# Even token blocks, weight sums on GpSimd and one more product summed in PSUM, in a kernel of attention and two dense layers

## The chip, the cores and the metric

The kernel runs on one core of a Trainium2 chip. The metric is the device time of one execution in microseconds (us). The profile names the engines PE (TensorE, matmuls), PEld (its weight loads), DVE (VectorE), ACT (ScalarE), POOL (GpSimd) and SP (SyncE, which issues nearly all DMAs here).

## The reference

Attention in two steps with batch 8, 8 heads, 576 tokens, head size 64 and 32 packed queries: `p_packed = softmax(p k^T) v`, then `out = softmax(q p_packed^T) p_packed`. The result is laid out as 4608 tokens of 512 values and goes through two blocks of the same shape, 512 to 2048 and back to 512:

```python
h = x @ w_in;  x = (h * np.cos(h)) @ w_out            # first block: layers one and two
h = x @ w2_in; g = h * np.tanh(np.log1p(np.exp(h)))   # second block: layers three and four
out = g @ w2_out
```

The second block's function is the activation that the kernel calls Mish. The weights of both blocks come as 64-bit floats and are turned into 32-bit ones in the kernel (an activation on ScalarE, a shift and a shift-or on VectorE).

## The kernel before

Every 32-bit product is made of three matmuls of a rounded type, high x high, high x low and low x high (`mm3`, L141). So each operand is split: ScalarE copies it to the rounded type, and VectorE or GpSimd subtracts that copy from it to get the low part.

**First part (L792 to L940).** The tokens run in 16 tiles of 288, each with 16 steps of 128 hidden columns, 256 steps in all. Step n does `l1(n)` (layer one into a PSUM bank of a ring of four), a chain on ScalarE and VectorE for h cos h (L809 to L833, the low part on GpSimd in L832), and `l2(n - 3)` (layer two into four accumulators). Attention, conversions of weights and preparations of the second block stand in tables `bg_pe`, `bg_ew` and `bg_ld` by step and are run between. One of these preparations is `wo2_pair` (L585): for each of eight pairs of 128 rows of w2_out it loads 64-bit data into two `raw` tiles, converts them (`conv2`), forms four differences in place (`sums`, L628, on VectorE), splits seven pieces (`piece`, L619 and L620) and writes each to DRAM (`tst`). Its steps are listed as offsets from a start step.

**Second part (L942 to L1138).** Layers three and four are each done with seven products of half-size blocks in place of eight (the Strassen-Winograd scheme). The tokens run in blocks: four of 1024 and one of 512 tokens, so that a half block has 512 or 256 columns (`n`). Per block, `x_load`, `x_sums` and `x_split` bring the seven combinations of x. They stand in the program behind the block before (`xs`, 18 units) and are let in one at a time between two groups.

For each of eight pairs of hidden columns (`p`), a block makes seven products for layer three (`product`, L947: six matmuls of `n` columns, `ps<-wab,ws` in the trace). K3 (L72) gives their order. The banks come from the ring of four, and VectorE adds them up (L1099, L1119) while ScalarE applies Mish. The third product is summed in PSUM on top of the first. The seven weight combinations of a pair are made in block 0: `comb_sums` (L556), then `ws_load` (L569), which splits the piece (L576 on ScalarE, L577 on VectorE, or on GpSimd for k = 2 and 5) and writes it to DRAM; later blocks load it from there. `ws_load` runs five products ahead, in five buffers that it shares with other temporary tiles.

Layer four has 56 groups per block (`group`, L1048), seven kinds `k` times eight `p`, each of two halves of three matmuls (`acc<-gh,T` in the trace). A group's operand is prepared by a possible sum (L1062) and a split (L961 on ScalarE, L962); its weights `T` are loaded from the pieces of `wo2_pair`, eight ahead. After each product one half of a group is taken from the queue (`sub`); behind the eight `p` the rest is done two halves at a time, until 28 halves are left over for the next block, and all of them in the last. After the eighth group of a kind `post` adds the bank to a sum (L1041) or writes a quarter of the result (L1015 transposes, L1018 DMAs).

The order on each engine isn't the program's order: the framework runs a timeline simulation of its own and issues each instruction at the place where that simulation has it ready, by priority. Each engine then executes its queue in that fixed order.

Of the kernel before, what the change touches and what calls it, by code (L numbers as in the profile page):

```python
# [12 lines left out]
ALU = mybir.AluOpType  # L13
# [57 lines left out]
HP_W = 400  # L71
K3 = (0, 2, 1, 3, 4, 5, 6)  # L72
K4 = (2, 7, 4, 5, 3)
# [11 lines left out]
def build(tc, q, k, v, p, w1i, w1o, w2i, w2o, out):  # L85
    nc = tc.nc
    ctx = ExitStack()
    with ctx:
# [480 lines left out]
        def ws_load(m):  # L569
            if m >= NQ:  # L570
                return
            p, k = divmod(m % 56, 7)
            k = K3[k]
            w = WS[m] = tp.tile([128, 2, 2, 128], F32R, tag="tmp", bufs=TMP_BUFS, name=nm("ws"))
            if m < 56:
                nc.scalar.copy(w[:, 0], CB[p][k])  # L576
                (nc.gpsimd if k % 3 == 2 else nc.vector).tensor_tensor(w[:, 1], CB[p][k], w[:, 0], ALU.subtract)  # L577
                d = WST[(p, k)] = dram.tile([128, 2, 2, 128], F32, name=nm("wst"))
                nc.sync.dma_start(d, w.bitcast(F32))
            else:  # L580
                nc.sync.dma_start(w.bitcast(F32), WST[(p, k)])
# [3 lines left out]
        def wo2_pair(p):  # L585
# [26 lines left out]
            def half(x, h):  # L612
                return raw[x][:, 256 * h : 256 * h + 256, 1].bitcast(F32)
# [12 lines left out]
            def sums(x, h, a, b):  # L626
                def f():
                    nc.vector.tensor_tensor(half(x, h), half(*a), half(*b), ALU.subtract)  # L628

                return f  # L630
# [4 lines left out]
                    (2, conv2(0)),  # L635
                    (3, conv2(1)),
                    (4, piece(1, 0, 0)),
                    (4, piece(2, 1, 0)),
                    (5, piece(3, 1, 1)),
                    (6, sums(0, 0, (0, 1), (0, 0))),  # L640
                    (6, sums(0, 1, (1, 1), (0, 1))),
                    (7, sums(1, 1, (1, 1), (0, 0))),
                    (7, sums(1, 0, (1, 0), (1, 1))),
                    (7, piece(5, 0, 0)),
                    (8, piece(7, 0, 1)),
                    (8, piece(6, 1, 1)),
                    (9, piece(4, 1, 0)),
                ],
# [212 lines left out]
        def x_load(i, a):  # L861
            def f():
                n = 1024 if i < 4 else 512
                if i == 0:
# [4 lines left out]
                for r, kc in zip(rs, (a, 2 + a)):  # L869
                    lo, hi = 1024 * i, 1024 * i + n  # L870
                    for t in range(lo // TT, (hi - 1) // TT + 1):
# [6 lines left out]
        def x_sums(i, a):  # L878
            def f():
                n = 512 if i < 4 else 256  # L880
                b1, b2 = raws[(i, a)]
# [10 lines left out]
        def x_split(i, a, k):  # L892
            def f():
                n = 512 if i < 4 else 256
                if a == 0:
# [104 lines left out]
        def block(i, n):  # L1000
            B = {"G": {}}
            r0 = 1024 * i

# [44 lines left out]
            def group(k, p):  # L1048
# [3 lines left out]
                def prep():  # L1052
# [12 lines left out]
                    g["hl"] = bp.tile([128, 2, BT], F32R, tag="gh2", bufs=4, name=nm("gh2"))  # L1065
                    split(g["hl"], src, n, nc.gpsimd if n < 512 and p % 4 == 3 else nc.vector)

# [20 lines left out]
            for p in range(8):  # L1088
# [20 lines left out]
                add(u3, prod(3), u2)  # L1109
                c = add(gb[:, 0, :n], prod(4), u3)  # L1110
                nc.scalar.activation(c, c, AF.Mish)
                ps = prod(5)
                a22 = add(ga[:, 1, :n], ps, u3)
                nc.scalar.activation(a22, a22, AF.Mish)
                add(u2, ps, u2)
                a21 = add(gb[:, 1, :n], prod(6), u2)
                nc.scalar.activation(a21, a21, AF.Mish)
# [10 lines left out]
        for i in range(NBLK):  # L1128
            n = 512 if i < 4 else 256
            xs = x_units(i + 1) if i < 4 else []  # L1130
# [31 lines left out]
```

## Time and profile before

| | us |
|---|---|
| median of three runs | 1584.92 |
| lowest, highest | 1582.02, 1586.48 |
| the profiled execution | 1589.55 |
| its span, first to last instruction | 1587.8 |
| mean granted TensorE clock, share of full speed | 0.981 |

The profile gives each engine's busy time, and the trace every instruction with its start, duration and what ended the idle time before it (`<-`). Matmuls overlap in a pipeline: a row's duration is longer than the distance to the next start. The second part begins at about 848 us. A window's row counts matmuls that touch the window.

### The profile page before, as it was taken

How to read it: one execution, taken by the hardware profiler on the slowest of the kernel's cores; microseconds unless marked ns; L12 is line 12 of the kernel's file. 1: busy time of each engine (PE TensorE's matmuls, PEld its weight loads, DVE VectorE, ACT ScalarE, POOL GpSimd, SP SyncE). 2: the span in 40 equal slices, each digit the busy share in tenths (PEclk: the TensorE clock that was granted, in tenths of full speed). 3: DMA queues.
4: the chain of work that ended last, by engine and by line, in shares of the span. 5: the costliest groups of instructions: out<-in, count | busy, mean ns of one | idle time of the engine just before them, and what ended most of it. 6: DMA issues, size and time to landing. Idle time of an engine off the chain costs nothing.

```text
span 1587.8 us, 28508 instructions
## 1 busy us (share of the span) xinstructions
PE 1488.5 (94%) x9728; PEld 1262.8 (80%) x9728; DVE 1159.0 (73%) x2284; ACT 895.9 (56%) x1822; POOL 423.4 (27%) x452
## 2 busy tenths in 40 slices
PE   3789999999998999999999989999999999999987
PEld 1577787799886899788998767888788878878877
DVE  4986767777677776687765889875986598657846
ACT  3676677666666677667665755433543444344433
POOL 0562323334443444456541112000100110010001
PEclk9889999999999999999999999999999999999999
DMA  9889666544547444532205858676867677767977
GB/s 282 284 217 226 174 160 161 136 125 111 150 125 193 121 122 126 153 115 69 96 16 180 255 204 254 209 222 194 249 206 221 203 225 214 217 199 228 273 256 245
DMA packets 243920, 294.45 MB, mean 185 GB/s; under 512 B 104000, under 2 KB 129088, under 8 KB 243776
## 3 DMA queue, kind: packets, MB, share of 16 engines
q1 hardware_dynamic: 243776, 292.63, 63.7%
q8 instruction: 77, 1.26, 0.3%
q14 instruction: 67, 0.55, 0.1%
HBM read 239.08 MB, written 53.48 MB: 184 GB/s over the span
## 4 chain that ended last, share of the span: by engine, by line
PE 55%; DVE 10%; DMA 6%; ACT 4%; issue 4%; POOL 1%; SPq 1%; DVEq 0%; POOLq 0%; ACTq 0%
PE acc L143 10%; PE acc L142 10%; PE acc L144 10%; PE ps L142 8%; PE ps L143 8%; PE ps L144 8%; DVE gh L962 1%; DMA xr<-x2d 1%; DVE r L815 1%; PE ps L488 1%; DMA tst<-wt 1%; DMA T<-tst 1%; DMA ws<-wst 1%; DVE t L1062 1%; DMA raw<-in_moe_w_in_dram 1%
## 5 line engine op out<-in xcount | busy, mean ns | idle before, releaser
L832 POOL TENSOR_TENSOR gh<-r,gh 128x288 fp32r<-128x288 f32 x256 | 214.6, 846 | 348.7 <-ACT gh L829 243.6
L143 PE MATMUL acc<-gh,wo 128*128 128x288 f32 x1024 | 302.6, 302 | 2.8 <-POOL gh L832 2.7
L144 PE MATMUL acc<-gh,wo 128*128 128x288 f32 x1024 | 299.4, 299 | 0.0
L142 PE MATMUL acc<-gh,wo 128*128 128x288 f32 x1024 | 277.9, 305 | 1.8 <-ACT gh L829 1.8
L142 PE MATMUL ps<-wab,ws 128*128 128x512 f32 (+1 forms) x560 | 209.4, 375 | 12.8 <-ACT m L1105 4.5
L142 PEld LDWEIGHTS acc<-gh,wo 128*128 128x128 f32 x1024 | 183.8, 192 | 32.3 <-ACT gh L829 9.0
L143 PE MATMUL ps<-wab,ws 128*128 128x512 f32 (+1 forms) x560 | 207.9, 371 | 0.8 <-DVE wab L899 0.8
L144 PE MATMUL ps<-wab,ws 128*128 128x512 f32 (+1 forms) x560 | 207.5, 371 | 1.0 <-DVE ws L577 1.0
L143 PE MATMUL acc<-gh,T 128*128 128x512 f32 (+1 forms) x560 | 206.5, 372 | 0.8 <-DVE gh L962 0.7
L143 PEld LDWEIGHTS acc<-gh,wo 128*128 128x128 f32 x1024 | 195.0, 191 | 14.5 <-issue 7.4
L144 PE MATMUL acc<-gh,T 128*128 128x512 f32 (+1 forms) x560 | 205.0, 370 | 0.0
L144 PEld LDWEIGHTS acc<-gh,wo 128*128 128x128 f32 x1024 | 195.1, 191 | 7.3 <-issue 7.3
L142 PE MATMUL acc<-gh,T 128*128 128x512 f32 (+1 forms) x560 | 179.7, 374 | 8.9 <-ACT gh L961 7.2
L821 ACT ACTIVATE r<-r,halfpi 128x288 f32<-128x288 f32 x256 | 136.1, 535 | 90.8 <-DVE r L815 89.5
L142 PE MATMUL ps<-aT,wab 128*128 128x288 f32 x512 | 161.4, 315 | 20.4 <-DVE r L822 18.1
L822 DVE TENSOR_TENSOR r<-r,ps 128x288 f32<-128x288 f32 x256 | 114.8, 450 | 72.9 <-ACT r L821 71.6
L812 ACT ACTIVATE ki<-ps,quarter 128x288 int32<-128x288 f32 x256 | 125.5, 497 | 66.6 <-PE ps L144 57.2
L814 DVE SCALAR_TENSOR_TENSOR r<-ki,ps 128x288 f32<-128x288 int32 x256 | 113.9, 447 | 58.7 <-ACT ki L812 45.1
L143 PE MATMUL ps<-aT,wab 128*128 128x288 f32 x512 | 154.2, 301 | 0.0
L144 PE MATMUL ps<-aT,wab 128*128 128x288 f32 x512 | 153.6, 300 | 0.0
L961 ACT CAST gh<-wo 128x512 fp32r<-128x512 f32 (+1 forms) x160 | 90.2, 577 | 105.3 <-PE acc L144 89.9
L962 DVE TENSOR_TENSOR gh<-wo,gh 128x512 fp32r<-128x512 f32 (+1 forms) x152 | 104.4, 696 | 59.7 <-ACT gh L961 59.0
(149 smaller groups left out, 2877.7 us busy)
## 6 DMA issues: line engine op xcount, KB each, us to landing
T<-tst SPq DMA_DIRECT2D x280, 256.0 KB, 3.4
ws<-wst SPq DMA_DIRECT2D x224, 256.0 KB, 3.0
kr<-in_k_dram SPq DMA_DIRECT2D x64, 272.0 KB, 5.8
ld<-ws SPq DMA_DIRECT2D x68, 256.0 KB, 3.4
kr<-in_q_dram SPq DMA_DIRECT2D x60, 272.0 KB, 5.5
tst<-wt SPq DMA_DIRECT2D x56, 256.0 KB, 2.6
wst<-ws SPq DMA_DIRECT2D x56, 256.0 KB, 3.1
x2d<-xo SPq DMA_DIRECT2D x64, 144.0 KB, 1.8
```

The source lines that it names most:

```text
L142: nc.tensor.matmul(ps, l0, r0, start=first, stop=False, skip_group_check=more)
L143: nc.tensor.matmul(ps, l0, r1, start=False, stop=False, skip_group_check=more)
L144: nc.tensor.matmul(ps, l1, r0, start=False, stop=last, skip_group_check=more)
L488: return nc.tensor.matmul(st[b][32 * l : 32 * l + 32], PK[(b, g)][r : r + 64, 32 * l : 32 * l + 32], ms[h // 2]["m"][r : r + 64], start=Tr ...
L812: nc.scalar.activation(ki, st["h"], AF.Identity, bias=quarter, scale=1.0 / TWO_PI)
L814: nc.vector.scalar_tensor_tensor(r, ki, -TWO_PI, st["h"], ALU.mult, ALU.add)
L815: (nc.gpsimd if n % C_MOD in C_POOL else nc.vector).tensor_scalar(r, r, 1.570796, -4.712388, ALU.min, ALU.max)
L821: nc.scalar.activation(g, g, AF.Sin, bias=halfpi, scale=1.0)
L822: nc.vector.tensor_tensor(g, g, st["h"], ALU.mult)
L832: nc.gpsimd.tensor_tensor(gh[:, 1], st["g"], gh[:, 0], ALU.subtract)
L961: nc.scalar.copy(hl[:, 0, :n], src)
L962: eng.tensor_tensor(hl[:, 1, :n], src, hl[:, 0, :n], ALU.subtract)
```

## The change

- The blocks of the second part become one of 1024 and four of 896 tokens (`N_BLK`, `R_BLK`): `n` is 512 in block 0 and 448 in the others. Loads, sums and splits of x follow.
- In `wo2_pair` the four differences are formed on GpSimd, and the list of steps is spread over offsets 2 to 18 instead of 2 to 9, with a sum or a piece at nearly every one.
- In `ws_load` all low parts of block 0's weights are made on GpSimd.
- In layer three the products at places 4 and 5 of K3 change places, and the seventh product is summed in PSUM on top of the fifth, after the sum for a22 has read it. One addition on VectorE per `p` goes.
- The low part of a group's operand is always made on VectorE; before, one group in four of the 256-column block had it on GpSimd.

```diff
@@ -69,7 +69,9 @@
 HP_CHAIN = 200
 HP_L1 = 150
 HP_W = 400
-K3 = (0, 2, 1, 3, 4, 5, 6)
+K3 = (0, 2, 1, 3, 5, 4, 6)
+N_BLK = (512, 448, 448, 448, 448)
+R_BLK = (0, 1024, 1920, 2816, 3712, 4608)
 K4 = (2, 7, 4, 5, 3)
 T_BUFS = 8
 T_AHEAD = 8
@@ -574,7 +576,7 @@
             w = WS[m] = tp.tile([128, 2, 2, 128], F32R, tag="tmp", bufs=TMP_BUFS, name=nm("ws"))
             if m < 56:
                 nc.scalar.copy(w[:, 0], CB[p][k])
-                (nc.gpsimd if k % 3 == 2 else nc.vector).tensor_tensor(w[:, 1], CB[p][k], w[:, 0], ALU.subtract)
+                nc.gpsimd.tensor_tensor(w[:, 1], CB[p][k], w[:, 0], ALU.subtract)
                 d = WST[(p, k)] = dram.tile([128, 2, 2, 128], F32, name=nm("wst"))
                 nc.sync.dma_start(d, w.bitcast(F32))
             else:
@@ -625,7 +627,7 @@
 
             def sums(x, h, a, b):
                 def f():
-                    nc.vector.tensor_tensor(half(x, h), half(*a), half(*b), ALU.subtract)
+                    nc.gpsimd.tensor_tensor(half(x, h), half(*a), half(*b), ALU.subtract)
 
                 return f
 
@@ -633,18 +635,18 @@
                 [load(0), load(1)],
                 [
                     (2, conv2(0)),
-                    (3, conv2(1)),
                     (4, piece(1, 0, 0)),
-                    (4, piece(2, 1, 0)),
-                    (5, piece(3, 1, 1)),
-                    (6, sums(0, 0, (0, 1), (0, 0))),
-                    (6, sums(0, 1, (1, 1), (0, 1))),
-                    (7, sums(1, 1, (1, 1), (0, 0))),
-                    (7, sums(1, 0, (1, 0), (1, 1))),
-                    (7, piece(5, 0, 0)),
-                    (8, piece(7, 0, 1)),
-                    (8, piece(6, 1, 1)),
-                    (9, piece(4, 1, 0)),
+                    (5, conv2(1)),
+                    (7, sums(0, 0, (0, 1), (0, 0))),
+                    (8, piece(2, 1, 0)),
+                    (10, sums(0, 1, (1, 1), (0, 1))),
+                    (11, piece(3, 1, 1)),
+                    (12, piece(5, 0, 0)),
+                    (13, sums(1, 1, (1, 1), (0, 0))),
+                    (14, piece(7, 0, 1)),
+                    (16, sums(1, 0, (1, 0), (1, 1))),
+                    (17, piece(6, 1, 1)),
+                    (18, piece(4, 1, 0)),
                 ],
             )
 
@@ -860,14 +862,14 @@
 
         def x_load(i, a):
             def f():
-                n = 1024 if i < 4 else 512
+                n = 2 * N_BLK[i]
                 if i == 0:
                     r = kr_tile([128, 2, 1024])
                     rs = [r[:, 0], r[:, 1]]
                 else:
                     rs = [tp.tile([128, n], F32, tag="raw", bufs=2, name=nm("xr")) for _ in range(2)]
                 for r, kc in zip(rs, (a, 2 + a)):
-                    lo, hi = 1024 * i, 1024 * i + n
+                    lo, hi = R_BLK[i], R_BLK[i + 1]
                     for t in range(lo // TT, (hi - 1) // TT + 1):
                         u, z = max(lo, t * TT), min(hi, t * TT + TT)
                         nc.sync.dma_start(r[:, u - lo : z - lo], x2d[t][:, kc, u - t * TT : z - t * TT])
@@ -877,7 +879,7 @@
 
         def x_sums(i, a):
             def f():
-                n = 512 if i < 4 else 256
+                n = N_BLK[i]
                 b1, b2 = raws[(i, a)]
                 b11, b12, b21, b22 = b1[:, :n], b1[:, n:], b2[:, :n], b2[:, n:]
                 t2, t3, t4 = [ld_tile([128, 512])[:, :n] for _ in range(3)]
@@ -891,7 +893,7 @@
 
         def x_split(i, a, k):
             def f():
-                n = 512 if i < 4 else 256
+                n = N_BLK[i]
                 if a == 0:
                     X[(i, k)] = wab_tile((0, 1, 0, 0, 0, 1, 1)[k], [128, 2, 2, 512], F32R)
                 x, src = X[(i, k)], raws[(i, a)][k]
@@ -999,7 +1001,7 @@
 
         def block(i, n):
             B = {"G": {}}
-            r0 = 1024 * i
+            r0 = R_BLK[i]
 
             def pair(c0):
                 return [psum.tile([128, 512], F32, tag=f"acc{c0 + c}", bufs=1, name=nm(f"acc{c0 + c}")) for c in range(2)]
@@ -1063,7 +1065,7 @@
                     else:
                         src = {1: a11, 2: a12, 4: a22, 6: s2}[k]
                     g["hl"] = bp.tile([128, 2, BT], F32R, tag="gh2", bufs=4, name=nm("gh2"))
-                    split(g["hl"], src, n, nc.gpsimd if n < 512 and p % 4 == 3 else nc.vector)
+                    split(g["hl"], src, n, nc.vector)
 
                 def item(c):
                     def run():
@@ -1107,13 +1109,13 @@
                 prod(2, px)
                 nc.scalar.activation(ga[:, 0, :n], px, AF.Mish)
                 add(u3, prod(3), u2)
-                c = add(gb[:, 0, :n], prod(4), u3)
+                pz = prod(4)
+                a22 = add(ga[:, 1, :n], pz, u3)
+                nc.scalar.activation(a22, a22, AF.Mish)
+                c = add(gb[:, 0, :n], prod(5), u3)
                 nc.scalar.activation(c, c, AF.Mish)
-                ps = prod(5)
-                a22 = add(ga[:, 1, :n], ps, u3)
-                nc.scalar.activation(a22, a22, AF.Mish)
-                add(u2, ps, u2)
-                a21 = add(gb[:, 1, :n], prod(6), u2)
+                prod(6, pz)
+                a21 = add(gb[:, 1, :n], pz, u2)
                 nc.scalar.activation(a21, a21, AF.Mish)
                 t = add(bt("t", 512, 2)[:, :n], a21, a22)
                 nc.vector.tensor_tensor(a21, t, ga[:, 0, :n], ALU.subtract)
@@ -1126,7 +1128,7 @@
             convs[(2, c)][0]()
         pump()
         for i in range(NBLK):
-            n = 512 if i < 4 else 256
+            n = N_BLK[i]
             xs = x_units(i + 1) if i < 4 else []
             block(i, n)
             keep = KEEP if i < 4 else 0
```

## Rows read from the trace of the kernel before

**Rows 1.** The page: busy us (share) xinstructions of each engine.
```profile
PE 1488.5 (94%) x9728; PEld 1262.8 (80%) x9728; DVE 1159.0 (73%) x2284; ACT 895.9 (56%) x1822; POOL 423.4 (27%) x452
```

**Rows 2.** Timeline of TensorE: start us, us, engine, line, operation, tiles, shape.
```profile
1404.96 0.39 PE L142 MATMUL acc<-gh,T 128*128 128x512 f32 x1
...
1423.10 0.39 PE L144 MATMUL acc<-gh,T 128*128 128x512 f32 x1
...
1478.29 0.28 PE L142 MATMUL ps<-wab,ws 128*128 128x256 f32 x1
...
1479.25 0.28 PE L144 MATMUL ps<-wab,ws 128*128 128x256 f32 x1
```

**Rows 3.** Windows: stretch, us, busy us (xinstructions), clock, DMA share, GB/s.
```profile
847.00:959.00 112.00, 102.67 (x428) 80.20 (x428) 92.27 (x167) 75.25 (x139) 19.93 (x19) 0.97 0.72 239
959.00:995.00 36.00, 35.42 (x152) 27.82 (x151) 32.73 (x51) 18.78 (x34) 9.07 (x5) 1.00 0.86 264
995.00:1110.00 115.00, 114.89 (x507) 94.78 (x506) 79.74 (x125) 45.35 (x77) 2.92 (x3) 1.00 0.70 205
1423.00:1456.00 33.00, 31.23 (x146) 25.30 (x145) 26.88 (x47) 16.03 (x32) 4.18 (x4) 0.95 0.71 217
1456.00:1536.00 80.00, 76.19 (x478) 69.29 (x477) 52.98 (x110) 29.00 (x65) 1.52 (x2) 0.96 0.88 275
1536.00:1582.00 46.00, 39.28 (x301) 36.79 (x300) 32.16 (x81) 19.66 (x52) 9.14 (x12) 1.00 0.81 250
...
340.00:760.00 420.00, 403.38 (x3275) 358.14 (x3274) 313.27 (x681) 285.17 (x627) 200.82 (x229) 0.98 0.49 134
```

**Rows 4.** Groups, TensorE, 1456:1583: xcount | busy us, mean ns | idle before.
```profile
L142 PE MATMUL ps<-wab,ws 128*128 128x256 f32 x98 | 28.8, 294 | 3.7 <-DMA ws<-wst 3.5
L142 PE MATMUL acc<-gh,T 128*128 128x256 f32 x112 | 25.3, 294 | 6.5 <-ACT gh L961 4.8 <-DMA T<-tst 1.3 <-DVE U L1041 0.3
```

**Rows 5.** Timeline of ScalarE; group of TensorE, 847:959.
```profile
935.36 0.62 ACT L898 CAST wab<-xr 128x512 fp32r<-128x512 f32 x1 [5.88 <-DMA xr<-x2d]
...
L142 PE MATMUL ps<-wab,ws 128*128 128x512 f32 x113 | 45.6, 404 | 7.5 <-ACT m L1105 4.2 <-ACT ws L576 1.9 <-DVE u L1099 0.6
```

**Rows 6.** Timeline, p = 3: fifth product ends, seventh starts, the add.
```profile
892.51 0.39 PE L144 MATMUL ps<-wab,ws 128*128 128x512 f32 x1
...
895.70 0.39 PE L142 MATMUL ps<-wab,ws 128*128 128x512 f32 x1
...
899.04 0.68 DVE L1099 TENSOR_TENSOR wo<-ps,u 128x512 f32<-128x512 f32 x1
```

**Rows 7.** Groups: VectorE and GpSimd 847:959, then VectorE 1159:1250.
```profile
L577 DVE TENSOR_TENSOR ws<-ld,ws 128x256 fp32r<-128x256 f32 x36 | 16.4, 459 | 1.7 <-ACT ws L576 1.7
L962 DVE TENSOR_TENSOR gh<-wo,gh 128x512 fp32r<-128x512 f32 x15 | 12.4, 827 | 0.0
...
L1119 DVE TENSOR_TENSOR wo<-t,wo 128x512 f32<-128x512 f32 x7 | 6.2, 883 | 0.1
...
L577 POOL TENSOR_TENSOR ws<-ld,ws 128x256 fp32r<-128x256 f32 x15 | 15.0, 998 | 92.2 <-ACT ws L576 76.3 <-DVE ld L563 8.4 <-DMA wst<-ws 7.6
...
L962 DVE TENSOR_TENSOR gh<-wo,gh 128x512 fp32r<-128x512 f32 x17 | 11.7, 691 | 13.8 <-ACT gh L961 13.6
...
L1119 DVE TENSOR_TENSOR wo<-t,wo 128x512 f32<-128x512 f32 x6 | 4.1, 683 | 0.1
```

**Rows 8.** Groups of VectorE, the whole trace.
```profile
L1099 DVE TENSOR_TENSOR wo<-ps,u 128x512 f32<-128x512 f32 x96 | 65.6, 684 | 29.4 <-PE ps L144 29.3
...
L628 DVE TENSOR_TENSOR raw<-raw 128x256 f32<-128x256 f32 x16 | 12.9, 808 | 2.1 <-POOL wt L620 2.1
...
L1099 DVE TENSOR_TENSOR wo<-ps,u 128x256 f32<-128x256 f32 x24 | 10.0, 422 | 6.6 <-PE ps L144 6.3
```

**Rows 9.** Timeline of the end.
```profile
1582.07 0.76 DVE L1041 TENSOR_TENSOR U<-acc,U 128x256 f32<-128x256 f32 x2 [1.74 <-PE acc L144]
```

**Rows 10.** Group of TensorE, 340:760.
```profile
L142 PE MATMUL ps<-aT,wab 128*128 128x288 f32 x278 | 87.4, 314 | 6.5 <-DVE r L822 5.5 <-ACT tmp L258 0.9
```

## The prediction

> **What bounds the kernel now.** I read the page's shares first: TensorE is busy 94% of the span, VectorE 73%, GpSimd 27%, and no other unit comes near the first [rows 1]. A busy share counts pipelined matmuls, so I then asked how far apart they start when nothing holds them: 81 matmuls of 512 columns run from 1404.96 to 1423.10, 80 steps of 0.227 us, and 8 steps of 256 columns take 0.96 us, 0.120 each [rows 2]. By a straight line through the two, 448 columns take 0.227 - 0.107/4 = 0.200 us.
>
> With these I went through the stages of the third layer [rows 3]. A stage's excess is its length less (matmuls x their step).
> - 995 to 1110, inside block 1: 507 x 0.227 = 115.1 of 115. No excess; DMA share 0.70, 205 GB/s.
> - 847 to 959, block 0: 428 x 0.227 = 97, excess 15; VectorE busy 92.3 of 112.
> - 959 to 995, block 1 coming in: 152 x 0.227 = 34.5 of 36, excess 1.5.
> - 1423 to 1456, the small block coming in: 42 of 256 columns and 104 of 512, 28.6 of 33, excess 4.4.
> - 1456 to 1582, the small block: 779 matmuls, 630 of them of 256 columns (three groups of 98, three of 112; one of each is shown [rows 4]) and 149 of 512: 75.6 + 33.8 = 109.4 of 126, excess 16.6. The DMA share is 0.88 at 275 GB/s in its first 80 us, and TensorE's waits there end on loads (ws 3.5, T 1.3 us) and on ScalarE's cast of gh (4.8 us) [rows 4].
>
> So TensorE bounds the full blocks without a gap, and the time to be won lies in block 0 (15 us), the small block (16.6 + 4.4) and the first two layers, where TensorE waits too but seldom.
>
> **The change, part by part.**
>
> *Even blocks.* Matmul work is the same: 672 matmuls a block, before 672 x (4 x 0.227 + 0.120), after 672 x (0.227 + 4 x 0.200), both 691 us. What goes is the stage in which the same weight bytes were fetched for half the columns. In a 448 block they are fetched in 0.88 of the time of a 512 block: 205/0.88 = 233 GB/s at a share of 0.80, under the 0.88 of the small block. VectorE keeps pace: 684 ns at 512 columns and 422 at 256 [rows 8] give 618 at 448, 0.90 of the time beside TensorE's 0.88. I take the inside of the last block as free of excess and leave 3 us for its end, where 42 groups run with no products between them and two of the results are added just before the same bank is used again: 16.6 to 3, **-13.5 us** (ends: -16.6, and -8 if half stays). The last block comes in like block 1, 4.4 to 1.5: **-3 us** (ends: -4.4 and 0; if the load of x in a 448 block meets the DMA limit, +3 in each of the four).
>
> *End of the kernel.* Behind the last matmul stand two adds, 0.76 us [rows 9], two transposes, taken as long, and four DMAs. At 448 columns each pair grows by 618/422, +0.35 us, and the bytes written by 1.75: **+1 us** (ends: +0.7 and +3).
>
> *Splits of block 0's weights on GpSimd.* Of 51 splits in this stage VectorE makes 36 at 459 ns, 16.5 us in all, and GpSimd 15 at 998 ns [rows 7]. All 36 move. What hides a later split is the five-deep ws buffer: a piece is asked for five products ahead (with the groups between them 5 x 9 x 0.227, some 10 us), and the split becomes 0.54 us longer. Behind it on GpSimd stand only further splits and the x splits, which wait for a load; that load already held ScalarE for 5.9 us and cost TensorE 4.3 [rows 5]. The relief of VectorE is smaller than 16.5 us: where both engines work, VectorE's instructions with two SBUF operands take longer, L962 827 ns against 691 in block 2, L1119 883 against 683 [rows 7]. Those two kinds lost 15 x 136 + 7 x 200 ns = 3.4 us beside 19 GpSimd instructions, at least 0.18 us for each; at most a whole 998 ns is lost. The 36 then cost VectorE 6.5 to 36 us; I take 15, nearer the measured end.
> The Trainium skill (SBUF — State Buffer, Who interferes with whom) says that a VectorE instruction with two SBUF inputs and a GpSimd instruction that reads SBUF exclude each other for the whole of one of them. The stretched L962 and L1119 agree; by the rule alone the move returns nothing, which is a rival below.
>
> *One product more in PSUM.* Per p VectorE loses one add of 684 ns [rows 8]; in block 0 8 x 0.68 = 5.4 us. With the splits (16.5 - 15) VectorE gets 7 of its 92 us back. The 15 us of block 0 have several causes, and 4.3 of them is the x load that no edit removes; I take **-3 us** (ends: -10.7 and +3). In the other blocks the saved add is beside a TensorE without gaps: 0.
> The accumulation adds a wait. The seventh product now writes the bank that the fifth filled, so it must wait until VectorE has read it (a22). Between them lie one product and two groups' halves, 2.7 us at 512 columns. In block 0 VectorE is later: for p = 3 the fifth product's last matmul starts at 892.51, the add runs from 899.04 to 899.72, and the seventh product began at 895.70, 4.0 us before that [rows 6]. Read the same way, p = 1 to 5 give 4.9, 2.3, 4.0, 2.5 and 2.2 us, 15.9 together. Before, four PSUM banks let TensorE run on. Behind the waiting matmul all of TensorE's queue stands; but once TensorE has waited, VectorE, busy 82% of this stage [rows 3], has caught up, so I don't count it for each p: **+4 us** (ends: 0 and +15.9). When a 448 block comes in VectorE is 32.7 of 36 us busy [rows 3], and TensorE fills the time with groups of the block before: 0.5 us for each of four, **+2 us** (ends: 0, and 4.0 each, +16).
>
> *Sums of the second weight on GpSimd, spread.* 32 sums leave VectorE, 25 us at 808 and 762 ns (one of the two kinds is shown [rows 8]), where an add of this size takes 0.42. They stood in bursts of four; from 340 to 760 us TensorE's l1 waited 5.5 us for L822 [rows 10]. Spreading removes the bursts; GpSimd, busy 201 of 420 us there [rows 3], gets some 30 more ahead of its gh splits, which run three steps ahead of their matmuls. **-2 us** (ends: -6, nearly all these waits, and +4, if gh comes late).
>
> Changes of the last block's splits from GpSimd to VectorE, of x's tile sizes and of the x pieces (four loads for five) go with the first part.
>
> **Sum:** -13.5 - 3 + 1 - 3 + 4 + 2 - 2 = -14.5 us. The profiled execution took 1589.55 us (span 1587.8), 4.6 above the median of 1584.92: 1575.0 by its own time, **1570 us** by the median's. The measurement tells about 0.3%, 4.8 us, from no change.
>
> **Rivals.**
> - *More relief.* Block 0 keeps only the 4.3 us of the x load (-11 for -3), the new wait costs nothing there, the first layers win 6: 1570 - 8 - 4 - 4 = 1554. For it: VectorE had 82% in block 0; against it: the longer instructions beside GpSimd. Chance 0.18.
> - *The excess moves.* The load of x meets the weight loads in each 448 block, and each comes in at 4.4 us like the small one: 4 x 2.9 = 11.6, 1582. For it: 0.86 share at 264 GB/s already at 959 to 995 [rows 3]; against it: only 1.5 us was lost there. Chance 0.13.
> - *The new wait decides (slower).* It is paid for every p in block 0 (15.9) and 4.0 us at each of four blocks' entries (16) instead of 6: 1570 + 26 = 1596. From 15 us more than I take, the gain is gone. For it: the add is late in six of eight p of block 0; against it: VectorE has spare time and TensorE other groups. Chance 0.10.
> - *GpSimd gives nothing back.* Each moved split holds VectorE for its 998 ns: 36 for 15 us, VectorE at 108 of 112 us in block 0, the relief of 3 turned into a loss of 14: 1587. For it: L1119's 200 ns; against it: most of VectorE's adds there read PSUM and stay at 680 ns. Chance 0.04. It is the skill's rule (same section) taken at its full length.
>
> **How the numbers follow.** The forecast has 0.55, with its own range of 1561 to 1579, all of it faster (under 1580.2). Faster: 0.55 + 0.18 + 0.03 of the second rival = 0.76. Same (to 1589.7): 0.10 of the second and 0.03 of the fourth = 0.13. Slower: 0.10 + 0.01 = 0.11. The range, 1553 to 1586, leaves out the slow rival and part of the fastest.
>
> **What would show it.** Right: in the last block matmuls of 448 columns 0.200 us apart with no load among TensorE's waits, DMA share near 0.80; L628 on GpSimd and no L577 on VectorE. The new wait shows as TensorE waiting at the seventh product for VectorE's add into wo; more than 10 us of it in block 0 makes step and forecast wrong. Steps of 448 columns well over 0.200 us, or waits for T or ws in all blocks, would make the largest term wrong.

## The result, and the profile after

The changed kernel takes 1594.28 us (median of 13 runs, 1590.5 to 1600.73) against 1584.49 for the kernel before on the same chip: ratio 1.0064, interval 1.0047 to 1.0081. It is slower by some 10 us; the forecast was 1570, with a range to 1586.

The profiled execution took 1598.11 us. From the page of after, the shares, which answer to [rows 1]:

```profile
PE 1497.5 (94%) x9728; PEld 1304.9 (82%) x9728; DVE 1115.9 (70%) x2186; ACT 908.3 (57%) x1830; POOL 475.4 (30%) x510
```

VectorE has 43 us less to do, GpSimd 52 more: the work moved as the diff says. TensorE's share is the same over a longer span, so it waits more. Windows of after, columns as in [rows 3]: block 0; the first 15 us of blocks 1 to 4 (counted by matmuls of products, 336 to a block, they begin at 948.2, 1099.5, 1244.3 and 1386.8), with two of the stretches between; and the start of the last stretch, where groups run without products:

```profile
837.00:948.00 111.00, 101.16 (x426) 81.35 (x425) 76.64 (x122) 82.77 (x144) 51.22 (x55) 0.97 0.75 246
948.00:963.00 15.00, 9.01 (x36) 6.35 (x35) 9.97 (x16) 8.08 (x15) 8.32 (x4) 0.98 0.60 170
...
1099.00:1114.00 15.00, 12.01 (x48) 9.27 (x47) 11.42 (x16) 8.06 (x16) 5.49 (x4) 0.89 0.67 202
1114.00:1244.00 130.00, 130.00 (x631) 118.08 (x630) 88.25 (x153) 52.61 (x96) 5.00 (x4) 1.00 0.77 234
1244.00:1259.00 15.00, 11.06 (x45) 9.12 (x44) 11.32 (x19) 8.05 (x16) 7.12 (x4) 0.89 0.64 200
1259.00:1387.00 128.00, 128.00 (x633) 118.65 (x632) 86.31 (x150) 52.35 (x96) 5.00 (x4) 1.00 0.78 237
1387.00:1402.00 15.00, 13.17 (x54) 10.56 (x54) 12.45 (x22) 9.15 (x19) 7.80 (x4) 0.89 0.61 184
...
1525.00:1540.00 15.00, 11.35 (x44) 9.89 (x43) 8.30 (x15) 5.80 (x11) 0.00 (x0) 0.77 0.26 75
```

Inside the blocks TensorE has no gap. At each entry it starts 36 to 54 matmuls in 15 us, where 15/0.203 = 74 fit, and behind the waits the granted clock drops: 0.89 over 15 us is 3.3 us at the lower level (1.2 of 2.4 GHz), some 1.6 us lost on top (in block 1 the drop falls behind the window). The same windows in the version without the second sum in PSUM (e_no_pz below, 1571.94 us):

```profile
843.00:947.00 104.00, 98.25 (x421) 77.33 (x420) 83.09 (x130) 71.98 (x135) 48.71 (x55) 1.00 0.76 256
947.00:962.00 15.00, 14.17 (x64) 11.40 (x63) 12.93 (x22) 9.80 (x20) 4.43 (x4) 1.00 0.73 217
1092.00:1107.00 15.00, 14.79 (x73) 13.25 (x72) 13.10 (x22) 9.91 (x21) 5.28 (x3) 1.00 0.74 232
...
1370.00:1385.00 15.00, 14.83 (x73) 13.13 (x72) 13.87 (x22) 9.65 (x20) 4.65 (x3) 1.00 0.82 248
1501.00:1516.00 15.00, 13.17 (x65) 11.75 (x64) 10.80 (x19) 7.84 (x15) 0.00 (x0) 1.00 0.38 107
```

64 to 73 matmuls at the entries, full clock throughout. To add it up I went through the starts of all matmuls from the first product to the last matmul; where a distance is more than 12 ns over n/2.4 + 13.3 ns (which fits 256, 384 and 512 columns), what it has over this sum counts as lost, all the rest as step (us; blocks counted as above; e_even, e_sums and e_pz follow below):

| | second part | steps | lost | by block |
|---|---|---|---|---|
| before | 734.2 | 690.6 | 43.6 | 15.5, 2.3, 2.0, 1.6, 22.2 |
| after | 751.9 | 702.9 | 49.0 | 14.7, 9.1, 5.7, 6.3, 13.3 |
| e_no_pz | 719.5 | 700.2 | 19.3 | 8.7, 1.4, 2.1, 1.9, 5.2 |
| e_even | 722.1 | 700.5 | 21.6 | 9.1, 2.0, 3.1, 2.2, 5.3 |
| e_sums | 734.6 | 690.7 | 43.9 | 9.5, 5.1, 2.4, 2.4, 24.5 |
| e_pz | 734.8 | 690.2 | 44.6 | 10.9, 3.5, 5.7, 5.1, 19.4 |

(The first part varies by 10 us between executions, and a single execution lies up to 9 us from its kernel's median, so these locate a loss; the ratios size it.)

How far one block can differ, block 0 shows: before and e_sums run the same instructions there in the same order on every engine, up to the border, and take 111.1 and 105.0 us. In e_sums ScalarE's wait for the next x is 3.30 us, not 5.88 [rows 5]:

```profile
924.34 0.62 ACT L898 CAST wab<-xr 128x512 fp32r<-128x512 f32 x1 [3.30 <-DMA xr<-x2d]
```

So some 6 of the 15 us that the prediction found in block 0 come and go between executions.

### The profile page after: what moved, and what is told of

Its sections match the earlier page's. It is cut to its first block, busy times and chain, and to the rows that moved or that the text cites. A ratio compares the mean times of both kernels' runs of the same rounds, so it can differ in the third digit from the quotient of the medians.

```text
span 1595.7 us, 28456 instructions
## 1 busy us (share of the span) xinstructions
PE 1497.5 (94%) x9728; PEld 1304.9 (82%) x9728; DVE 1115.9 (70%) x2186; ACT 908.3 (57%) x1830; POOL 475.4 (30%) x510
## 5 line engine op out<-in xcount | busy, mean ns | idle before, releaser
L144 PE MATMUL ps<-wab,ws 128*128 128x448 f32 (+1 forms) x560 | 207.7, 378 | 17.3 <-ACT wo L1110 5.7
L145 PE MATMUL ps<-wab,ws 128*128 128x448 f32 (+1 forms) x560 | 211.3, 377 | 6.9 <-POOL wab L901 4.8
L145 PE MATMUL acc<-gh,T 128*128 128x448 f32 (+1 forms) x560 | 210.5, 376 | 1.0 <-DVE gh L964 1.0
L146 PE MATMUL acc<-gh,T 128*128 128x448 f32 (+1 forms) x560 | 209.6, 375 | 0.0
L146 PE MATMUL ps<-wab,ws 128*128 128x448 f32 (+1 forms) x560 | 208.9, 375 | 0.0
L145 PEld LDWEIGHTS acc<-gh,wo 128*128 128x128 f32 x1024 | 193.4, 189 | 13.6 <-issue 8.5
L144 PE MATMUL acc<-gh,T 128*128 128x448 f32 (+1 forms) x560 | 183.7, 378 | 4.7 <-ACT gh L963 4.3
L824 DVE TENSOR_TENSOR r<-r,ps 128x288 f32<-128x288 f32 x256 | 114.7, 450 | 76.6 <-ACT r L823 75.9
L963 ACT CAST gh<-wo 128x448 fp32r<-128x448 f32 (+1 forms) x160 | 90.4, 578 | 107.6 <-PE acc L146 83.6
L964 DVE TENSOR_TENSOR gh<-wo,gh 128x448 fp32r<-128x448 f32 (+1 forms) x160 | 102.4, 649 | 52.1 <-ACT gh L963 51.4
```

The costliest lines, as they stand in the source:

```text
L144: nc.tensor.matmul(ps, l0, r0, start=first, stop=False, skip_group_check=more)
L145: nc.tensor.matmul(ps, l0, r1, start=False, stop=False, skip_group_check=more)
L146: nc.tensor.matmul(ps, l1, r0, start=False, stop=last, skip_group_check=more)
L824: nc.vector.tensor_tensor(g, g, st["h"], ALU.mult)
L963: nc.scalar.copy(hl[:, 0, :n], src)
L964: eng.tensor_tensor(hl[:, 1, :n], src, hl[:, 0, :n], ALU.subtract)
```

## The experiments

All ratios are to the kernel before, run beside them on the same chip; its median was 1583.8 to 1587.3 us. A ratio is an estimate over all runs beside each other and can lie 0.2% from the quotient of two medians. The diffs show only the lines that decide.

**The step of 448 columns by itself** (m_steps): matmuls of nine widths, back to back and behind a wait.

```diff
+        for n in (512, 448, 256, 480, 384, 416, 288, 320, 352):
+            ps = run(n)
```

> Leaves the whole computation out: only matmuls like those of the third layer (six to a product, a weight load for each, four banks in turn), 144 of each width from 256 to 512 columns, first back to back, then each width behind a wait for VectorE. Theory: the distance of starts isn't a straight line in the columns; 448 columns take 0.203 to 0.207 us here too, with no other engine at work, against 0.227 at 512 and 0.120 at 256, and the value may differ before and after a wait. Rival: 448 columns take 0.200 us here and the longer steps of the changed kernel come from the traffic of the other engines or the DMAs.

Its timeline of TensorE: first and last of 144 matmuls of 448 columns, then of 384.

```profile
110.45 0.36 PE L35 MATMUL ps<-x,ws 128*128 128x448 f32 x1
...
139.44 0.36 PE L37 MATMUL ps<-x,ws 128*128 128x448 f32 x1
...
188.12 0.34 PE L35 MATMUL ps<-x,ws 128*128 128x384 f32 x1
...
212.91 0.33 PE L37 MATMUL ps<-x,ws 128*128 128x384 f32 x1
```

143 steps each: 0.2027 us for 448 columns and 0.1734 for 384. The line through 256 and 512 gives 0.200 and 0.1733: 384 lies on it, 448 doesn't. Behind one of two waits 448 took 0.2067, behind the other 0.203 again.

**The parts alone.** Even blocks (e_even), spread sums (e_sums), both (e_es):

```diff
+N_BLK = (512, 448, 448, 448, 448)         # e_even; with it sizes and splits as in the change
...
-                nc.vector.tensor_tensor(half(x, h), half(*a), half(*b), ALU.subtract)
+                nc.gpsimd.tensor_tensor(half(x, h), half(*a), half(*b), ALU.subtract)   # e_sums; with it the spread list
```

> The kernel before with the even blocks alone (512 and four of 448 columns, low parts of the groups all on VectorE). Theory that the even blocks lose by the step of 448 columns (0.205 for the 0.200 expected, 2688 matmuls, 12.6 us) and by stalls at each block's entry what they gain in the last block (8 us): the first part ends at 848 us as before, the time is 1588 to 1594. Rival that the even blocks gain and the GpSimd splits with the new wait cost: 1570 to 1575.

> The kernel before with the sums of the second output weight on GpSimd and spread over the steps, nothing else. Theory: this alone makes the first part 11 us shorter, which ends near 837 us, and the second part stays 734 us long to its last matmul: 1573. Rival: the first part got shorter because the order of the whole program changed with the other edits too; then it ends between 840 and 848 us and the time is 1577 to 1585.

> The kernel before with the even blocks and the spread sums on GpSimd alone. If the two gains add (0.9943 and 0.996): 0.990, 1571. If the changed order takes one of them back: 0.994 or more.

Measured: 0.9943 [0.9923, 0.9964], 0.9960 [0.9939, 0.9981] and 0.9906 [0.9881, 0.9931]. Both parts gain, and the gains add. That even blocks would lose was a miss, and of the sums the rival came out (1580.65 us, the second part from 841.1).

**The other parts undone in the changed kernel.** Old block sizes (e_old_blocks), no second sum in PSUM and the old order of products (e_no_pz), splits of block 0 as before (e_no_ws):

```diff
+N_BLK = (512, 512, 512, 512, 256)          # e_old_blocks
...
+K3 = (0, 2, 1, 3, 4, 5, 6)                 # e_no_pz
...
+                add(u2, ps, u2)
+                a21 = add(gb[:, 1, :n], prod(6), u2)
...
+                (nc.gpsimd if k % 3 == 2 else nc.vector).tensor_tensor(w[:, 1], ...)   # e_no_ws
```

> The changed kernel with the block sizes of before (four of 1024 tokens, one of 512). Theory of the step: the first part stays 11 us shorter (ends near 837), block 0 costs 0 to 4 us more by the new wait or the splits, 1573 to 1578. Rival that splits and new wait cost: 1590 or more.

> The changed kernel without the seventh product's summing in PSUM (order of products and sums in layer three as before). Theory that this part costs the time, by the stalls at each block's entry and the clock drops behind them: the stalls of the second part fall from 49 us to 22 to 28, ratio to before 0.987 to 0.992 (about 1570). Rival that the GpSimd splits of block 0 cost: stays above 1.000.

> The changed kernel with block 0's weight splits on VectorE and GpSimd as before. Theory that the summing in PSUM costs the time: stays at 1.002 to 1.007 with the stalls at the entries of blocks 1 to 4 as in the changed kernel (5 to 9 us each). Rival that the GpSimd splits cost: 0.987 to 0.992.

Measured: 0.9991 [0.9977, 1.0005], a miss; 0.9910 [0.9891, 0.9929]; 1.0051 [1.0030, 1.0072]. So the edit with the second sum costs 0.9910 to 1.0064, 24 us, and turns a gain of 14 us into the loss. The splits change nothing that these ratios can tell: 0.9910 with them, 0.9906 without, 1.0064 and 1.0051 in the changed kernel.

**Order or sum** (e_k3: new order, but no sum in PSUM), **the order of x's pieces** (e_xorder), **the edit in the kernel before** (e_pz):

```diff
-                pz = prod(4)                # e_k3
+                ps = prod(4)
...
+                add(u2, ps, u2)
...
-                prod(6, pz)
-                a21 = add(gb[:, 1, :n], pz, u2)
+                a21 = add(gb[:, 1, :n], prod(6), u2)
...
-  [x_split(i, a, k) for k in range(7)]      # e_xorder
+  [x_split(i, a, k) for k in (K3 if i else range(7))]
```

> The changed kernel with its new order of layer three's products, but the seventh product in a bank of its own and the third addition back on VectorE (no second sum in PSUM). Theory A, the accumulation costs (TensorE waits for the read of the fifth product's bank, and that bank is held over two products): then this kernel comes to where the version without the PSUM edit came, 0.991 of the kernel before (about 1571 us), with under 25 us of TensorE's waits in the second part. Theory B, the new order of the products costs: it stays at 1.004 to 1.007 (about 1593 us), with 40 us of waits and more. A value of 0.996 to 1.000 means that each has a part.

> The changed kernel, but the pieces of x for blocks 1 to 4 are split in the order in which the products use them (0, 2, 1, 3, 5, 4, 6; before in the order of their numbers, so that the piece of the fifth product was split after one that is needed later). Theory A, the price of the PSUM edit lies at the entries of the blocks and comes from this late piece: the waits in the first 20 us of blocks 2 to 4 fall from about 5 us each to 2, and the ratio to the kernel before falls from 1.0064 to 0.997 to 1.001. Theory B, it comes from the bank that is held and from the order of TensorE's queue: the ratio stays at 1.004 to 1.008.

> The kernel before with nothing but the second sum in PSUM and its order of the products; blocks of 1024 and 512 tokens as before. Theory A, the edit costs in any block: it is slower by about what it cost in the changed kernel, ratio 1.006 to 1.016 (about 1595 to 1610 us). Theory B, it costs only together with the blocks of 896 tokens, where an entry has less time: ratio 0.997 to 1.004, since the version with old block sizes and all other edits stood at 0.9991.

Measured: 0.9979 [0.9962, 0.9995], so order and sum each have a part; 1.0069 [1.0047, 1.0092], so late pieces of x aren't the cause; 1.0010 [0.9991, 1.0029], nearly free in the old blocks. The entries lose 1.2, 3.7 and 3.5 us more there too, block 0 and the small block 4.6 and 2.8 less than in before's trace; beside e_sums, though, block 0 loses 1.4 more, so no gain is shown there. Why the old blocks pay so little is open.

**Where the edit costs.** The changed kernel with the edit in some pairs only:

```diff
+def summed(i, p):
+    return i == 0                 # e_pz_b0
+    return i > 0 and p == 0       # e_pz_entry
+    return i > 0 and p > 0        # e_pz_late
+    return i > 0 and p < 7        # e_pz_mid
+    return i > 0 and p == 7       # e_pz_last
```

> The changed kernel with the second sum in PSUM and its order of products in block 0 only; the other four blocks keep the old order, with the third addition on VectorE. Theory A, the cost lies in block 0 and at the entries of blocks 1 to 4: block 0 takes about 7 us more than without the edit (111.4 us from its first product to the next block's, against 104.3), with 19 loads of an activation table on ScalarE in place of 11, and the ratio to the kernel before is 0.994 to 0.997 (0.991 without the edit, 1.0064 with all of it). Theory B, the bank that is held costs a little for every pair of every block: one fifth of the cost, 0.993 to 0.995, with no more loads of tables. Theory C, block 0 gains (one addition less for VectorE, the bound that the prediction saw there): 0.987 to 0.990.

> The changed kernel with the second sum in PSUM and its order of products only for the first pair of hidden columns of blocks 1 to 4, the pair that runs while a block comes in; block 0 and the other pairs keep the old order. Theory A, the cost lies in block 0 and at the entries: stalls of 2 us and more at the entries, each with a stretch of half clock behind it, and a ratio of 0.996 to 1.001. Theory B, the held bank costs for every pair: 4 of 40 pairs, ratio 0.991 to 0.993.

> The changed kernel with the second sum in PSUM and its order of products only for pairs 1 to 7 of blocks 1 to 4, where TensorE runs without gaps; block 0 and the first pairs keep the old order. Theory A: neither cost nor gain there, ratio 0.990 to 0.993. Theory B, the held bank costs for every pair (28 of 40): 1.000 to 1.003. The price of block 0 alone, of the entries and of the rest together should make the 1.5% of the whole edit, if they add.

> The changed kernel with the second sum in PSUM and its order of products only for pairs 0 to 6 of blocks 1 to 4; block 0 and the last pair of each block keep the old order. Theory A, the loss outside block 0 comes from the last pair (its seventh product waits for VectorE and falls behind the next block's first products, whose loads and splits then come late): no stalls over 1 us at the entries, ratio 0.986 to 0.991. Theory B, the bank and the five-deep weight buffer are held a little too long in every pair, and the block's entry only shows the sum: 24 of the 28 pairs, ratio 0.998 to 1.001.

> The changed kernel with the second sum in PSUM and its order of products only for the last pair (7) of blocks 1 to 4. Theory A: these four pairs carry the loss, stalls of about 2 us with half clock behind them at the entries of blocks 2 to 4, ratio 0.997 to 1.002. Theory B: 4 of 40 pairs, ratio 0.990 to 0.993.

| pairs with the edit | ratio | interval |
|---|---|---|
| none | 0.9910 | 0.9891 to 0.9929 |
| block 0 | 0.9964 | 0.9944 to 0.9985 |
| first pair, blocks 1 to 4 | 0.9879 | 0.9858 to 0.9901 |
| pairs 1 to 7 | 1.0014 | 0.9998 to 1.0030 |
| pairs 0 to 6 | 0.9904 | 0.9889 to 0.9920 |
| the last pair alone | 1.0062 | 1.0044 to 1.0080 |
| all | 1.0064 | 1.0047 to 1.0081 |

I had put the cost at the first pair, which runs while the block comes in: wrong, it costs nothing. Pairs 1 to 7 then came out where theory B of that run stood (the bank costs for every pair), and the run without the last pair refuted B. Four of the 40 pairs, the last of blocks 1 to 4, cost as much as all, and 28 pairs nothing. (The prices don't add: block 0 and the last pairs alone would make 2%, and pairs 1 to 7 cost less than the last of them alone. Why is open.) Groups of TensorE in the first 12 us of block 2, first without the edit in the last pair (e_pz_mid), then with it there alone (e_pz_last):

```profile
L152 PE MATMUL acc<-gh,T 128*128 128x448 f32 x9 | 3.3, 366 | 0.0
L153 PE MATMUL acc<-gh,T 128*128 128x448 f32 x9 | 3.3, 365 | 0.0
...
L151 PE MATMUL acc<-gh,T 128*128 128x448 f32 x10 | 2.8, 381 | 0.9 <-ACT gh L970 0.9
```

```profile
L152 PE MATMUL ps<-wab,ws 128*128 128x448 f32 x8 | 3.9, 489 | 0.9 <-POOL wab L908 0.8 <-DVE wab L908 0.2
...
L151 PE MATMUL ps<-wab,ws 128*128 128x448 f32 x9 | 3.7, 435 | 1.4 <-DMA ws<-wst 1.2 <-ACT wab L907 0.2
L152 PE MATMUL acc<-gh,T 128*128 128x448 f32 x3 | 1.1, 367 | 0.0
L153 PE MATMUL acc<-gh,T 128*128 128x448 f32 x3 | 1.1, 366 | 0.0
L151 PE MATMUL acc<-gh,T 128*128 128x448 f32 x4 | 1.0, 363 | 0.0
```

Products: 25 matmuls in the one, 26 in the other. What is missing is what fills TensorE while x comes in: 28 matmuls of groups against 10.

The reason begins inside a block. The wait lets the framework put the next pair's first product ahead of a pair's seventh. In after, pairs 6 and 7 of block 1: ScalarE copies pair 7's first product (m) before VectorE has pair 6's seventh for its last addition (a21):

```profile
1086.56 0.53 ACT L1107 COPY m<-ps 128x448 f32<-128x448 f32 x1 [1.60 <-PE ps L146]
...
1088.18 0.62 DVE L1101 TENSOR_TENSOR wo<-ps,u 128x448 f32<-128x448 f32 x1 [3.83 <-PE ps L146]
```

In after the copy starts ahead of the addition behind 31 of the 35 pairs that have another behind them in their block, in e_no_pz and in e_k3 behind 5: the sum does it, not the order of K3. Behind a last pair it is the next block's first product that goes ahead. VectorE's timeline says what follows. In e_pz_mid (first product of block 2 at 1087.78):

```profile
1086.16 0.62 DVE L1108 TENSOR_TENSOR wo<-ps,u 128x448 f32<-128x448 f32 x1 [0.67 <-PE ps L153]
1089.31 1.21 DVE L1108 TENSOR_TENSOR t<-wo,wo 128x448 f32<-128x448 f32 x1 [2.53 <-ACT wo L1135]
...
1092.22 1.70 DVE L971 TENSOR_TENSOR gh<-wo,gh 128x448 fp32r<-128x448 f32 x3
1093.84 0.62 DVE L893 TENSOR_TENSOR ld<-xr,xr 128x448 f32<-128x448 f32 x1
```

and in e_pz_last (the block by count from 1091.3):

```profile
1092.70 0.62 DVE L1108 TENSOR_TENSOR wo<-ps,u 128x448 f32<-128x448 f32 x1 [3.43 <-PE ps L153]
1095.84 0.63 DVE L893 TENSOR_TENSOR ld<-xr,xr 128x448 f32<-128x448 f32 x1 [2.51 <-DMA xr<-x2d]
1096.38 0.62 DVE L1108 TENSOR_TENSOR t<-wo,wo 128x448 f32<-128x448 f32 x1
...
1103.23 1.68 DVE L971 TENSOR_TENSOR gh<-wo,gh 128x448 fp32r<-128x448 f32 x3
```

TensorE's products at this border of e_pz_last:

```profile
1089.66 0.37 PE L151 MATMUL ps<-wab,ws 128*128 128x448 f32 x1
...
1091.29 0.36 PE L151 MATMUL ps<-wab,ws 128*128 128x448 f32 x1
```

The a21 of 1092.70 starts as the last matmul of the second of these ends, so that one is the old pair's seventh product and the first, at 1089.66, is the new block's (its copy m waits behind casts of x). The pair's last addition thus runs 1.6 us before the new block's first product in e_pz_mid and 3.0 behind it in e_pz_last. By then the sums of the new x stand ahead of `t` in VectorE's queue, and the first of them waits 2.5 us for its load. The groups' splits come 13.6 us behind the first product, not 4.4, and all groups behind that pair's queue up with them. The loads come late too: SyncE issues the first of that x's eight loads at 1087.23, 2.4 us before the first product, in e_pz_mid at 1082.14, 5.6 before. What the late addition and the late loads cost each wasn't tried apart. After shows the same: a21 at 1100.95 behind a wait of 3.84 us for the product, the first x sum at 1103.21, `t` at 1104.82. In block 4 the last 42 groups wait too: TensorE stands for 3.65 us at 1533.6, and the clock is 0.77 in after's last row above, 1.00 in e_no_pz's.

**A version from this** (e_384: even blocks and spread sums with widths on the line; e_384_mid: with all edits of the changed kernel, the second sum only in pairs 0 to 6 of blocks 1 to 4):

```diff
-N_BLK = (512, 448, 448, 448, 448)
+N_BLK = (512, 512, 512, 384, 384)
```

> As the run with even blocks and spread sums, but with blocks of 512, 512, 512, 384 and 384 columns. By the steps measured alone (0.2267 and 0.1734 us) the matmuls of the second part take 672 x (3 x 0.2267 + 2 x 0.1734) = 690 us for 701 with 448 columns: 10 to 12 us shorter than that run if the loads keep up. Rival: at 384 columns the weights are fetched in 0.76 of a 512 block's time, 205/0.76 = 270 GB/s, as much as the small block of before drew, and waits on loads take the 10 us back.

> A candidate: blocks of 1024, 1024, 1024, 768 and 768 tokens (512 and 384 columns), sums and splits on GpSimd as changed, the second sum in PSUM only for pairs 0 to 6 of blocks 1 to 4. The same blocks without any second sum stood at 0.9857. Theory A: VectorE's spared additions there are beside a TensorE without gaps, worth 0 to 0.4%: 0.982 to 0.987. Theory B, every summed pair costs: 0.990 or more.

Measured: 0.9857 [0.9835, 0.9879] and 0.9857 [0.9835, 0.9878], 1563.99 and 1558.63 us: faster than both kernels. The second sum, here together with the splits on GpSimd, is worth nothing even where it costs nothing. Steps give 672 x (3 x 0.227 + 2 x 0.1734) = 691 us against 700 with 448 columns; of these 9 to 10 us, 7.8 were measured (0.9906 to 0.9857).

## Why the prediction was wrong

**The new wait: this step failed.** It was priced at +4 in block 0 and +2 at the entries, on the ground that "once TensorE has waited, VectorE [...] has caught up". With the order of products that goes with it, it cost 24 us (0.9910 to 1.0064). In the table, after loses 6.0 us more than e_no_pz in block 0 and 23.8 more in blocks 1 to 4. I had looked for TensorE standing at the seventh product. The framework instead puts the next pair's first products ahead of that product, inside a block at no cost (pairs 0 to 6: 0.9904). Behind the last pair the next products are those of the next block, and what came late was the pair's last sum, the groups that hang on it, the loads of x, and the clock. The rival "the new wait decides" named 1596, near the time, partly by luck: it had the entries (16 us), but through TensorE waiting for that bank, and 15.9 in block 0 for a wait in each pair. (It also counts six late additions in block 0; the readings give five.)

In block 0 I counted VectorE. Its relief came, 76.6 us of 111 busy against 92.3 of 112 [rows 3], and the block got no shorter (111.4 us for 111.1, and for e_sums' 105.0): TensorE waits for ScalarE. Table loads of ScalarE in block 0 of after, then of e_no_pz:

```profile
L551 ACT ACT_TABLE_LOAD x9 | 11.5, 1283 | 0.2
...
L1110 ACT ACT_TABLE_LOAD x6 | 7.7, 1283 | 0.1
...
L1119 ACT ACT_TABLE_LOAD x3 | 3.8, 1283 | 0.1
...
L1114 ACT ACT_TABLE_LOAD x1 | 1.3, 1283 | 0.0
```

```profile
L1110 ACT ACT_TABLE_LOAD x6 | 7.7, 1283 | 0.1
L551 ACT ACT_TABLE_LOAD x5 | 6.4, 1283 | 0.1
```

With a21 delayed, its Mish falls between conversions of weights, which use another table: 19 loads for 11, 10.3 us of ScalarE. (The Trainium skill, ScalarE activation tables: per-element evaluation and per-set limits, What a function is on this engine, puts two functions of different sets one load of 1283 ns apart; the trace agrees.) One place, ScalarE and then TensorE in after:

```profile
882.91 1.28 ACT L1119 ACT_TABLE_LOAD   x1
...
884.85 1.28 ACT L551 ACT_TABLE_LOAD   x1
...
887.11 1.28 ACT L1110 ACT_TABLE_LOAD   x1
888.41 0.60 ACT L1110 ACTIVATE wo<-ps 128x512 f32<-128x512 f32 x1
```

```profile
885.38 0.40 PE L146 MATMUL ps<-wab,ws 128*128 128x512 f32 x1
889.06 0.49 PE L144 MATMUL ps<-wab,ws 128*128 128x512 f32 x1 [3.28 <-ACT wo L1110]
```

Three loads stand before the Mish that frees a bank, and TensorE loses 3.4 us. Such waits make 5.7 us in this block; the ratio puts the edit in block 0 alone at 0.54%, 8.6 us. The loads aren't all of it: e_no_ws and e_pz, with the edit but the splits as before, have 19 loads too, and their block 0 takes 106.7 us each. With all splits on GpSimd as well it takes 110.3 to 112.2 (four traces); without the second sum in block 0, 103.1 to 105.6 (eleven traces, before's left out), wherever the splits are. By these traces some 4 us come only from the two edits together; through what isn't shown.

**Even blocks: right in sign, two sizes off.** Alone they gave 0.57%, 9.0 us, for the 15.5 of the sum. The step "by a straight line" of 0.200 was mis-sized: after's blocks run without a gap at 130/631 = 0.206 and 128/633 = 0.202 us a matmul, 2 to 6 ns more on each of 2688. In e_even that is 700.5 us of steps for 690.6, 10 us lost: this term was mis-sized too. Against that, 43.6 us of losses became 21.6, 22 for the 16.5 that I took. The last block came out as forecast, 22.2 to 5.3 with its entry, and no load stands among TensorE's waits in it. The DMA share inside the blocks was 0.77 and 0.78 at 234 and 237 GB/s, for 0.80 at 233; TensorE's products and groups with a wait in after's block 4:

```profile
L144 PE MATMUL acc<-gh,T 128*128 128x448 f32 x194 | 62.5, 380 | 4.7 <-ACT gh L963 4.3 <-issue 0.3
...
L144 PE MATMUL ps<-wab,ws 128*128 128x448 f32 x111 | 40.9, 374 | 1.8 <-DVE t L1101 1.8
```

Some 6 us more are block 0, 15.5 to 9.1, and can't be put down to the edit: e_sums, with the old blocks, loses 9.5 there. ScalarE's wait of 5.88 us for the x load [rows 5], of which I had written that "no edit removes" its cost, is 1.90 in e_even and 3.30 in e_sums: it was in part that execution's.

```profile
928.97 0.57 ACT L900 CAST wab<-xr 128x448 fp32r<-128x448 f32 x1 [1.90 <-DMA xr<-x2d]
```

**End of the kernel: right.** Two adds of 1.16 us for 0.76 [rows 9], and from the last matmul to the end 6.9 us for 5.8: +1.1 for +1.

```profile
1588.74 1.16 DVE L1043 TENSOR_TENSOR U<-acc,U 128x448 f32<-128x448 f32 x2 [1.29 <-PE acc L146]
```

**Splits on GpSimd: right that no time comes back, wrong in the reason.** Groups in block 0, of after and of e_no_ws, answering to [rows 7]:

```profile
L579 POOL TENSOR_TENSOR ws<-ld,ws 128x256 fp32r<-128x256 f32 x51 | 45.8, 909 | 60.5 <-ACT ws L578 57.7 <-POOL ws L579 1.6 <-DVE ld L563 1.2
...
L1121 DVE TENSOR_TENSOR wo<-t,wo 128x512 f32<-128x512 f32 x7 | 7.8, 1111 | 0.1
```

```profile
L579 DVE TENSOR_TENSOR ws<-ld,ws 128x256 fp32r<-128x256 f32 x37 | 16.3, 443 | 1.5 <-ACT ws L578 1.5
...
L1121 DVE TENSOR_TENSOR wo<-t,wo 128x512 f32<-128x512 f32 x7 | 5.3, 761 | 0.0
```

VectorE is rid of 16.3 us, and its other instructions in the block lose 5.7 in all, L1121 alone 7 x 350 ns = 2.5; its busy time there falls from 83.9 to 76.6 us. I had taken 15 of 16.5 as lost. So relief is real, and the rival by which each moved split holds VectorE for its whole length falls (its 108 us should also read 106). (The Trainium skill, SBUF — State Buffer, Who interferes with whom, has a VectorE instruction with two SBUF inputs and a GpSimd one that reads SBUF exclude each other: the longer L1121 agrees, and the sum over 51 splits does not come near their 45.8 us.) It brings no time: without the second sum in block 0 the block is as long with the splits on either engine, so VectorE isn't what it waits for.

**Sums on GpSimd: right in sign, too small.** 0.40%, 6.3 us, for 2. Not from the waits that I named: l1 waits 6.7 us for that addition in e_sums and 5.4 in after, 5.5 before [rows 10]. From 340 to 760 us e_sums starts 3326 matmuls for 3275 [rows 3], at a clock of 0.99 for 0.98 and with 11.7 us less on VectorE:

```profile
340.00:760.00 420.00, 409.06 (x3326) 361.81 (x3325) 301.58 (x662) 289.32 (x633) 222.80 (x257) 0.99 0.47 129
```

Which of many small waits went stays open.

**The sum without the failed step** would have been 1570 - 6 = 1564 us; e_no_pz at 0.9910 is 1570.7 by the same median. What is left of the miss is above all the step of 448 columns, about 10 us, less the gains that were larger than forecast, such as the sums'.

Open: what the order costs by itself (0.9979; in e_k3 the seventh products aren't overtaken any more than in e_no_pz), and why the edit is nearly free with the old blocks.

## What to carry to other kernels

Where an engine's queue is put in order by readiness, a new wait needn't be paid where it stands: follow what is moved ahead of it, and ask what the last round before a stage's border hands to the next stage. An edit that pays nothing inside a stage can still cost at the border; try it with the last round left out before judging it. Measure the step of a new tile width before interpolating between two known ones. Before a stage's loss goes into a sum, see it in a second execution: one stage here lost 15 us in one trace and 9 in another with the same queues.

## What the runs showed of the hardware

- Matmuls of 448 columns back to back take 0.2027 us, 0.2067 behind some waits; blocks 2 and 4 of after keep the longer value nearly throughout, block 3 the shorter. 384 columns take 0.1734, on the line of 256 and 512. What picks the value is open.
- At the entries of after, 0.3 to 1.1 us behind the end of idle times of TensorE of 1.8 to 2.8 us, the granted clock fell to the lower level (1.2 of 2.4 GHz) for some 3.4 us, 0.89 over 15 us. In the last stretch TensorE stood 1.83 us for `gh` both in e_pz_mid and in e_no_pz: the clock fell likewise in the one (0.89 over 15 us) and stayed at 1.00 in the other. The length of the idle time alone doesn't tell.
